# A fused long convolution and spectral mixing layer on one core: output tiles by threes ahead of two U tiles, and x's last piece in quarters

## The chip, the cores and the metric

The kernel runs on one core of one Trainium2 chip. The metric is the device time of one execution in microseconds (us). Three runs of the kernel before gave 373.09, 373.68 and 374.57 us, a median of 373.68. The execution that the profiler recorded took 373.66 us; its span, from the first to the last recorded work, is 371.9 us.

## The reference

Two layers follow one another. The first is a causal convolution of each channel of `x` (8 batches of 5696 positions and 128 channels) with a filter `h` as long as the sequence. The second is a Fourier mixing layer: the 64 lowest modes of the sequence are multiplied by complex 128 x 128 matrices and added back, and a gated linear map closes it.

```python
B, S, D = x.shape                      # 8, 5696, 128
L = 2 * S
Xf = np.fft.rfft(x, n=L, axis=1)
Hf = np.fft.rfft(h, n=L, axis=0)
x = np.fft.irfft(Xf * Hf[None], n=L, axis=1)[:, :S, :]       # the first layer

X = np.fft.rfft(x, axis=1)                                   # the second
Xr, Xi = np.real(X[:, :64]), np.imag(X[:, :64])
Yr = einsum('bmd,mde->bme', Xr, w_r) - einsum('bmd,mde->bme', Xi, w_i)
Yi = einsum('bmd,mde->bme', Xr, w_i) + einsum('bmd,mde->bme', Xi, w_r)
y = np.fft.irfft(Y, n=S, axis=1)       # Y holds Yr + i Yi in its first 64 modes
u = x + y
out = u + np.maximum(u @ w_ch, 0.0)
```

The result is 8 x 5696 x 128 in float32. All matmuls of the kernel take float16.

## The kernel before, in words

The sequence is cut as 5696 = 89 x 64, so that the long Fourier transform becomes two short ones, all done as matmuls with constant matrices. The eight batches are worked in four pairs, g = 0 to 3.

A recorder writes the program down first. Every operation is given an engine, the tokens that it reads and the tokens that it writes, and each engine runs its list strictly in the order of the recording; an operation waits on semaphores for the writers of what it reads and the readers of what it overwrites. There is no scheduler: the order of the recording calls is the order of the work on every engine. DMAs are recorded on the lists of SyncE or GpSimd and are issued when their turn comes. Most instructions carry the line of a helper in the profile: L330 is every matmul, L318 and L320 evictions on ScalarE, L322 and L324 evictions on VectorE, L327 every DMA.

The stages, in order:

- Start. The filter `h` and the first pair of `x` are loaded; `x` comes in eight pieces into the raw tiles `Xr`, each piece by two DMAs (L363). VectorE places each piece into `Xin` (function `x_place`, L370), where the 128 channels stand as four groups of 32 columns. Meanwhile TensorE transforms the filter (`a_tile`'s sister loop and `filter_couple`), and where it has nothing to do it runs matmuls on a constant whose result nobody reads (`idle`, L425). The eight `x_place` calls stand at L703, an `idle(18, 6)` at L707. Then 32 column tiles of `x` are transformed (`a_tile`, L466); tile j takes columns 4j to 4j + 3, all from the column group j // 8, but waits for all eight placed pieces as a whole (`XIN`).
- For each pair: the second short transform, the product with the filter's spectrum on VectorE, the third stage, which writes its results (`Zs`, `Zt`) to the scratch tensor `zscr` in HBM, and the 64 modes. Between two pairs the column tiles of the next one are worked.
- The modes are mixed with `W` and transposed into `C` (L820 to L847).
- The last stage, from 256 us of the span to its end, is where most of the change lies. A pair has 4 chunks of 16 rows for each of its 2 batches, and each chunk 2 halves: 16 U tiles per pair. A U tile (`u_tile`, L800) is 2 matmuls of 356 columns with `C` and 16 of 89 columns with the `zscr` data that was loaded back (tiles `ZT`, five chunk buffers), added up in two PSUM banks; one copy then moves it into `UT` on ScalarE or VectorE. When all 8 U tiles of a batch are there, the output tiles of that batch can be worked: 12 O tiles (`o_tile`, L857), 11 full ones with 512 positions and a short one with 64. A full O tile is 4 matmuls of 256 columns, whose right side `WI` is `w_ch` beside the identity; ScalarE takes the relu of one half into `R` (L886), VectorE adds the other half to it in float32 (L887), and SyncE stores it. Two O tiles side by side make one 512 KB store ("wide"); the eleventh full tile makes a store of 256 KB, the short one 32 KB.

U and O tiles share four PSUM slots of two banks each, taken in turn (`LSLOT = [0, 2, 4, 6]`). A tile can therefore start on TensorE only when the tile four before it has been read out: a U tile by its copy, an O tile by both the relu and the add.

The O tiles of one pair are worked between the U tiles of the next. Before, the loop at L903 put one O tile behind the first half of each chunk and two behind the second: U O U O O. For the last pair the batches come one after the other, with two O tiles behind each U tile and, for its second batch, two and three in turn; O tiles of the last pair's first batch join the list when its 8 U tiles are done. The last 12 O tiles follow the last U tile. Which engine copies a U tile out was counted off: five of eight on ScalarE, three on VectorE. When both batches of a chunk are done, its buffer is loaded again for the chunk five further on (`load_zt`, L913), after the O tiles of that chunk on SyncE's list.

Of the kernel before, what the change touches and what calls it, by code (L numbers as in the profile page):

```python
# [123 lines left out]
def bass_long_conv_fft__then__afno_spectral_mix_kernel(nc, x, h, moe_w_r, moe_w_i, moe_w_ch, out):  # L124
    B, S, D = x.shape
# [3 lines left out]
    NQ = S // J  # L129
# [12 lines left out]
    f1 = np.zeros((P, 2 * NK))  # L142
# [65 lines left out]
    def at(name, cols, dt, off):  # L208
        return nc.alloc_sbuf_tensor_at(name, [P, cols], dt, offset=off)
# [11 lines left out]
    XD = D // 4  # L221
    XE = XD + 2
    XQ = 2 * J * XE
    XW = 4 * XQ
    a_x = take(XW * 2)
    x_sb = at("Xin", XW, F16, a_x)
# [16 lines left out]
    XC = 4  # L243
    XN = J // XC
    XB = XN * D
    x_raw = [at(f"Xr{i}", XB, F16, a_as + 2 * HPW + 2 * XB * i if i < 7 else a_st + 2 * J * D) for i in range(2 * XC)]
# [15 lines left out]
    NC = 5  # L262
# [29 lines left out]
    def ap(t, row, p0, n, off, dims):  # L292
        return bass.AP(t, p0 * row + off, [[row, n]] + [list(d) for d in dims])
# [5 lines left out]
    def pv(bank, off, dims, p0=0, n=P):  # L299
        return bass.AP(ps, p0 * 4096 + bank * 512 + off, [[4096, n]] + [list(d) for d in dims])  # L300

    R = Recorder(nc)
# [3 lines left out]
    def bank(i):  # L306
        return ("bank", i)
# [21 lines left out]
    def mm(o, l, r, st, sp, reads, writes):  # L329
        R.add("tensor", lambda h_: h_.matmul(o, l, r, start=st, stop=sp), reads, writes)  # L330
# [3 lines left out]
    def once(key, toks):  # L334
        if key in first:
            return []
        first[key] = 1
        return list(toks)
# [3 lines left out]
    def turns(name, items):  # L342
        i = ring2.get(name, 0)
        ring2[name] = i + 1
        return items[i % len(items)]
# [24 lines left out]
    def x_place(i, src, toks):  # L370
        R.add("vector", lambda e: e.tensor_copy(bass.AP(x_sb, i * XN * XE, [[XW, NQ], [XE, XN], [XQ, 4], [1, XD]]),
                                                bass.AP(src, 0, [[XB, NQ], [D, XN], [XD, 4], [1, XD]])),
              list(toks) + XZ, [("xin", i)])

    def w_pieces():
        out_ = []
# [27 lines left out]
        return ((k // KP) ^ c) * MC + k % KP * 3 * J + (J if r == 0 else 0)  # L404

    XZ = [("xz", 0), ("xz", 1)]
    XIN = [("xin", i) for i in range(2 * XC)]
    XR = [[("xr", i, p_) for p_ in range(2)] for i in range(2 * XC)]
    GP = 2 * KT
    NS = NK // 2 + 1  # L410
# [14 lines left out]
    def idle(n, b0, w=512):  # L425
        for i in range(n):
            mm(pv(b0 + i % 2, 0, [[1, w]]), f1_sb[:, 0:P], ap(f1_sb, 2 * NK, 0, P, 0, [[0, w // P], [1, P]]),
               True, True, [("f1",)], [bank(b0 + i % 2)])
# [12 lines left out]
    for c_ in (0, 2, 1, 3):  # L441
        dst = bass.AP(hp_sb, c_ // 2 * J * HS + c_ % 2 * DC, [[HPW, NQ], [HS, J], [1, DC]])
        src = bass.AP(h_in, c_ * DC, [[J * D, NQ], [D, J], [1, DC]])
# [8 lines left out]
    for j in range(16):  # L452
        t = turns("h", [0, 2, 4, 6])
        for i in range(4):
            d = 4 * j + i
# [10 lines left out]
    def a_tile(j, slots, eng=None):  # L466
        t = turns("s", slots) if len(slots) > 1 else slots[0]
        for i in range(4):
            d = 4 * j + i
            mm(pv(t + i // 2, (i % 2) * 2 * NK, [[1, 2 * NK]]),  # L470
               ap(x_sb, XW, 0, P, d // XD * XQ + d % XD, [[XE, 2 * J]]), f1_sb[:, :], True, True,
               XIN + XZ + [("f1",), ("xc", d // XD)], [bank(t + i // 2)])
        if eng == "both":
            for i, e in enumerate(("vector", "scalar")):
                evac(bass.AP(a_sb, 4 * j + 2 * i, [[AW, P], [D, 2 * NK], [1, 2]]), pv(t + i, 0, [[1, 2 * NK], [2 * NK, 2]]),
                     [bank(t + i)], [("as", j + i)], 1.0 / 64, eng=e, after=once(("hp", j), HP))
            return
        evac(bass.AP(a_sb, 4 * j, [[AW, P], [D, 2 * NK], [2, 2], [1, 2]]),
             pv(t, 0, [[1, 2 * NK], [512, 2], [2 * NK, 2]]),
             [bank(t), bank(t + 1)], [("as", j)], 1.0 / 64, eng=eng, after=once(("hp", j), HP))  # L480
# [78 lines left out]
    V, A = "vector", "scalar"  # L559
# [140 lines left out]
    for c_ in range(NE):  # L700
        filter_couple(c_, turns("f", SLOTS[0:3]), "vector" if c_ == 1 else "scalar")
        idle(1, 6)
    for i in range(2 * XC):  # L703
        x_place(i, x_raw[i], XR[i])
    for i in (4, 5):
        m_cross(i, "gpsimd")
    idle(18, 6)  # L707
    load.update(scalar=0.0, vector=0.0)
    for j in range(32):
        a_tile(j, [turns("s", SLOTS)], "both" if j == 31 else share(720))  # L710
        if j >= 10 and j % 5 == 0:
            c_ = NE + (j - 10) // 5
# [8 lines left out]
    for g_ in range(NP):  # L721
# [27 lines left out]
        if g_ + 1 < NP:  # L749
            for j in range(4, 32):  # L750
# [3 lines left out]
                if wp and j > 4 and j % 2 == 1:  # L754
                    dst, src_, ring, tok = wp.pop(0)
# [11 lines left out]

    LSLOT = [0, 2, 4, 6]
    NCH = J // ZB
    n_ev = [0]  # L770
    ahead = {}

    def u_z(i, b, half, alone=False, parts=(0, 1)):
# [23 lines left out]
           ib_sb[:, (c_ * ZB + pl0) * NQ:(c_ * ZB + pl0 + 4) * NQ], first_, not first_,  # L797
           [("c", g_ // 2), ("ib", 0)] + ([("ib", 1)] if c_ >= NCH // 2 else []), [bank(t + hb)])

    def u_tile(i, b, half):  # L800
        g_, c_ = divmod(i, NCH)
        t = ahead.get((i, b, half))
        if t is None:
            t = u_z(i, b, half)
        else:
            for hb in range(2):
                u_c(i, b, half, t, hb, False)
        ub = (g_ % 2) * 2 + b
        old = {0: WT, 1: WT, 2: U_ALL, 3: U_ALL}[ub]
        n_ev[0] += 1  # L810
        e = "scalar" if n_ev[0] % 8 in (0, 2, 3, 5, 7) else "vector"
        src = pv(t, 0, [[1, NQ], [512, 2], [NQ, 4]])
        evac(bass.AP(u_sb[ub], c_ * ZB + half * 8, [[S, P], [J, NQ], [4, 2], [1, 4]]),
             src, [bank(t), bank(t + 1)], [("u_", ub, 2 * c_ + half)], eng=e, after=once(("u", ub), old))
# [39 lines left out]
    NW = S // P  # L854
    TAIL = S - NW * P

    def o_tile(g_, b, r4):  # L857
        ub = (g_ % 2) * 2 + b
        bb = 2 * g_ + b
        t = turns("l", LSLOT)  # L860
        i = n_o[0]
        n_o[0] += 1
        full = r4 < NW // 4
        last_ = (g_, b) == (NP - 1, 1)
        wide = r4 < (8 if last_ else NW // 4 // 2 * 2)
        big = wide or (last_ and full)
        h_ = r4 % 2 if wide else 0
        if big:
            if not h_:
                o_cur[0] = turns("o8", list(range(NO8)))  # L870
            ob, key, old = o8_sb[o_cur[0]], ("o8", o_cur[0]), o8_old[o_cur[0]]
        else:
            k_ = turns("os", list(range(NO)))
            ob, key, old = o_sb[k_], ("os", k_), o_old[k_]
        OW = 1024 if big else 512
        n, rows = (4, P) if full else (1, TAIL)
        rd = [("u_", ub, c_) for c_ in range(2 * NCH)] + [("wch",), ("i16",)]
        for j in range(n):
            lh = bass.AP(u_sb[ub], 4 * r4 + j, [[S, P], [NW, P]]) if full else u_sb[ub][:, NW * P:S]
            mm(pv(t + j // 2, (j % 2) * 256, [[1, 256]], 0, rows), lh, WI, True, True, rd, [bank(t + j // 2)])  # L880
        bk = [bank(t), bank(t + 1)] if full else [bank(t)]
        rs = r_sb[i % NR]
        rv = bass.AP(rs, 0, [[512, rows], [P, n], [1, P]])
        ov = bass.AP(ob, h_ * 512, [[OW, rows], [P, n], [1, P]])
        src_r, src_u = pv(t, 0, [[256, n], [1, P]], 0, rows), pv(t, P, [[256, n], [1, P]], 0, rows)
        R.add("scalar", lambda e: e.activation(rv, src_r, RELU), bk, [("r", i % NR)], after=once(("r", i % NR), G_ALL + XTT + [("y", q) for q in range(4)] + [("id",)]))  # L886
        R.add("vector", lambda e: e.tensor_tensor(ov, src_u, rv, ADD), bk + [("r", i % NR)],  # L887
              [key + (h_,)], after=once(key, old))
        if wide and not h_:
            return  # L890
        w_ = (2 if wide else 1) * 4 * D
        if full:
            dst = bass.AP(out.tensor, out.offset + bb * S * D + (4 * r4 - 4 * h_) * D, [[NW * D, P], [1, w_]])
            src = ob[:, 0:w_]
        else:
            dst = bass.AP(out.tensor, out.offset + bb * S * D + NW * P * D, [[D, TAIL], [1, D]])
            src = ob[0:TAIL, 0:P]
        dma("sync", dst, src, "o", [key + (v_,) for v_ in range(h_ + 1)])

    todo = []  # L900
    NB = NCH * NP
    NW4 = NW // 4 + 1
    for g_ in range(NP):  # L903
        last = g_ == NP - 1
        order = [(c_, b) for b in range(2) for c_ in range(NCH)] if last else [(c_, b) for c_ in range(NCH) for b in range(2)]
        for n, (c_, b) in enumerate(order):
            i = NCH * g_ + c_
            for half in range(2):
                u_tile(i, b, half)
                for _ in range((2, 2 + half)[n >= NCH] if last else 1 + half):  # L910
                    if todo:
                        o_tile(*todo.pop(0))
            if b == 1 and i + NC < NB:  # L913
                load_zt(i + NC)
            if last and n == NCH - 1:
                todo += [(g_, 0, r4) for r4 in range(NW4)]
        todo += [(g_, b, r4) for b in range(1 if last else 0, 2) for r4 in range(NW4)]
    while todo:
        o_tile(*todo.pop(0))
    R.add("sync", lambda e: e.nop(), [], [("o8", i, v_) for i in range(NO8) for v_ in range(2)] + [("os", i, 0) for i in range(NO)])  # L920
# [31 lines left out]
```

## Time and profile before

| what | before |
|---|---|
| median of three runs | 373.68 us |
| the profiled execution, its time | 373.66 us |
| its span | 371.9 us |
| TensorE busy, matmuls | 353.4 us, 95% |
| ScalarE busy | 312.5 us, 84% |
| VectorE busy | 300.6 us, 81% |
| GpSimd busy | 97.2 us, 26% |
| HBM read and written | 68.4 and 51.1 MB |

The busy shares are means over stages with different limits. Matmuls are pipelined, so the duration of one is longer than the distance to the next; where a rate matters, the distance between starts is read. PEld is the weight load that goes with each matmul, and runs ahead of it. In the rows of the timeline the first number is the start and the second the length in us; what stands in brackets is how long the engine was idle before it, and what released it.

### The profile page before, as it was taken

To read this page: it belongs to the slowest core of one execution; us is meant where nothing else is said; L and a number is where in the kernel's file an instruction comes from. 1 tells how busy PE (TensorE), PEld (TensorE's weight loads), DVE (VectorE), ACT (ScalarE), POOL (GpSimd) and SP (SyncE) were. 2 spreads that over 40 slices of the span, in tenths; PEclk is the share of its full clock that TensorE was granted. 3 is DMA by queue.
4 is the path that set the end of the run, shared out by engine and by line. 5 is a ranking of instruction groups with operands and counts; after the bars stand their busy time and mean duration, and the time that the engine had idled before them with its cause. 6 is when DMAs were issued, how large, how long until landed. Compare 5 with 4: busy or idle time off the path is not lost.

```text
span 371.9 us, 12188 instructions
## 1 busy us (share of the span) xinstructions
PE 353.4 (95%) x5222; PEld 268.0 (72%) x5222; DVE 300.6 (81%) x333; ACT 312.5 (84%) x492; POOL 97.2 (26%) x140
## 2 busy tenths in 40 slices
PE   7989989999999999899999899999999999999992
PEld 3756866667856668766668666668898898888872
DVE  7786988999889999889999987873356776778784
ACT  8875989999999999899999899994477767677783
POOL 8865013211922313723305204336000000000000
PEclk9999999999999999999999999999999999999998
DMA  7998579998999997999998989999999999998677
GB/s 141 285 221 219 117 163 254 279 254 235 144 142 239 249 256 159 151 164 236 250 267 131 360 236 341 349 314 367 401 399 374 403 420 406 405 403 357 275 276 297
DMA packets 84129, 101.71 MB, mean 273 GB/s; under 512 B 22078, under 2 KB 68926, under 8 KB 81106
## 3 DMA queue, kind: packets, MB, share of 16 engines
q1 hardware_dynamic: 59643, 67.73, 53.3%
q0 software_dynamic: 24432, 33.20, 43.4%
q8 instruction: 41, 0.67, 0.7%
q14 instruction: 13, 0.11, 0.1%
HBM read 68.38 MB, written 51.12 MB: 321 GB/s over the span
## 4 chain that ended last, share of the span: by engine, by line
PE 79%; ACT 13%; DMA 3%; DVE 2%; issue 1%; DVEq 0%; POOL 0%; POOLq 0%
PE ps L330 79%; ACT As L320 9%; DMA Hin<-in_h_dram 3%; DVE U L623 1%; ACT R L886 1%; ACT UT L318 1%; ACT Hp L445 1%; DVE Ah L324 0%; DVE UT L322 0%; ACT Ah L320 0%; ACT Hs L318 0%; DVE O L887 0%; DVEq L105 0%; POOL Hin L327 0%; ACT C L320 0%
## 5 line engine op out<-in xcount | busy, mean ns | idle before, releaser
L330 PE MATMUL ps<-U,Wc 128*128 128x512 f16 (+1 forms) x368 | 94.6, 376 | 0.0
L631 DVE TENSOR_TENSOR U<-Xs,Hs 128x2048 f16<-128x2048 f16 (+1 forms) x68 | 80.5, 1188 | 10.9 <-ACT Xs L318 8.8
L318 ACT CAST Xs<-ps 128x1024 f16<-128x1024 f32 (+1 forms) x72 | 69.5, 971 | 6.9 <-PE ps L330 4.7
L887 DVE TENSOR_TENSOR O<-ps,R 128x512 f32<-128x512 f32 x81 | 52.5, 686 | 20.4 <-ACT R L886 11.2
L318 ACT CAST Zs<-ps 128x512 f16<-128x512 f32 (+1 forms) x120 | 62.9, 600 | 0.4
L886 ACT ACTIVATE R<-ps 128x512 f32<-128x512 f32 x96 | 50.9, 573 | 14.4 <-PE ps L330 14.0
L324 DVE TENSOR_SCALAR As<-ps 128x720 f16<-128x720 f32 (+1 forms) x65 | 53.8, 881 | 4.6 <-PE ps L330 3.4
L330 PE MATMUL ps<-As,M 64*128 64x128 f16 x1440 | 48.7, 217 | 4.8 <-DVE U L623 3.5
L330 PE MATMUL ps<-WI,UT 128*128 128x256 f16 x360 | 51.7, 278 | 0.5 <-DVE O L887 0.4
L330 PE MATMUL ps<-F,Xin 128*128 128x180 f16 x512 | 51.3, 248 | 0.5 <-ACT As L320 0.2
L320 ACT ACTIVATE As<-ps 128x720 f16<-128x720 f32 (+1 forms) x67 | 46.3, 763 | 4.3 <-PE ps L330 4.0
L330 PEld LDWEIGHTS ps<-F,Xin 128*128 128x128 f16 x512 | 43.6, 142 | 8.4 <-ACT As L320 1.5
L330 PEld LDWEIGHTS ps<-U,Wc 128*128 128x128 f16 x368 | 28.4, 97 | 27.6 <-ACT Zs L318 4.8
L330 PEld LDWEIGHTS ps<-As,M 64*128 64x128 f16 x1440 | 40.3, 94 | 10.6 <-DVE U L623 4.2
L631 DVE TENSOR_TENSOR U<-ps,Hs 128x2048 f16<-128x2048 f32 x20 | 45.7, 2284 | 0.0
L318 ACT CAST UT<-ps 128x712 f16<-128x712 f32 x40 | 30.0, 752 | 17.4 <-PE ps L330 16.4
L327 POOL DMA_DIRECT2D Xt<-in_x_dram x48 | 24.7, 518 | 75.6 <-PE ps L330 74.9
L330 PEld LDWEIGHTS ps<-WI,UT 128*128 128x128 f16 x360 | 39.2, 152 | 4.1 <-issue 1.9
L330 PE MATMUL ps<-IBs,C 128*128 128x356 f16 x128 | 39.2, 314 | 0.8
L330 PEld LDWEIGHTS ps<-G,Zs 128*128 128x128 f16 x468 | 25.4, 96 | 12.0
L318 ACT CAST Zt<-ps 128x512 f16<-128x512 f32 (+1 forms) x64 | 33.8, 606 | 0.1
L322 DVE CAST UT<-ps 128x712 f16<-128x712 f32 x24 | 21.4, 891 | 9.5 <-PE ps L330 9.5
(90 smaller groups left out, 506.8 us busy)
## 6 DMA issues: line engine op xcount, KB each, us to landing
out_dram<-O SPq DMA_DIRECT2D x39, 512.0 KB, 7.4
zscr<-Zs SPq DMA_DIRECT2D x57, 256.0 KB, 6.0
zscr<-Zt SPq DMA_DIRECT2D x31, 256.0 KB, 7.3
Xt<-in_x_dram POOLq DMA_DIRECT2D x24, 320.0 KB, 6.5
W<-wscr POOLq DMA_DIRECT2D x8, 512.0 KB, 8.7
ZT0a<-zscr SPq DMA_DIRECT2D x3, 1024.0 KB, 9.8
Xr<-in_x_dram POOLq DMA_DIRECT2D x8, 320.0 KB, 15.9
M<-cM POOLq DMA_DIRECT2D x3, 720.0 KB, 12.8
```

What stands on the lines that cost most here:

```text
L318: R.add(e, lambda h_: h_.copy(dst, src), reads, writes, after=after)
L320: R.add(e, lambda h_: h_.activation(dst, src, COPY, scale=scale), reads, writes, after=after)
L322: R.add(e, lambda h_: h_.tensor_copy(dst, src), reads, writes, after=after)
L324: R.add(e, lambda h_: h_.tensor_scalar_mul(dst, src, scale), reads, writes, after=after)
L327: R.add(eng, lambda h_: h_.dma_start(dst, src), reads, writes, ring=ring, after=after)
L330: R.add("tensor", lambda h_: h_.matmul(o, l, r, start=st, stop=sp), reads, writes)
L445: R.add("scalar", lambda e, dst=dst, src=src: e.copy(dst, src), HT, [("hp", c_)])
L623: R.add("vector", lambda e, b=b, s_=s_: e.tensor_tensor(bass.AP(u_s[i], b * 512, [[2048, P], [1024, 2], [1, n * D]]), s_, hv, MULT), [tok, ...
L631: R.add("vector", lambda e: e.tensor_tensor(uv, src, hv, MULT), bk + [("h", t, 0), ("h", t, 1, 0), ("h", t, 1, J)], [("u", i)])
L886: R.add("scalar", lambda e: e.activation(rv, src_r, RELU), bk, [("r", i % NR)], after=once(("r", i % NR), G_ALL + XTT + [("y", q) for q in ...
L887: R.add("vector", lambda e: e.tensor_tensor(ov, src_u, rv, ADD), bk + [("r", i % NR)], [key + (h_,)], after=once(key, old))
```

## The change

Four things are changed, and one follows.

1. The last stage's order is written out. For pairs 1 to 3 as far as they work output tiles: three O tiles, then two U tiles (`PLAN`, with "A" a U tile copied by ScalarE and "V" one copied by VectorE). In pair 0 there are no O tiles yet, so its U tiles follow each other and alternate between the two engines. For the last pair the order is `LAST_PLAN`, with 12 groups of 2, 3 or 4 O tiles and one or two U tiles; 11 of its 16 U tiles are copied by ScalarE.
2. The reload of a chunk buffer is recorded directly behind the chunk's last U tile.
3. In the very last batch the ninth and tenth O tiles are stored as one wide pair like the others, and the short tile comes ahead of the eleventh.
4. The last of the eight pieces of the first `x` is placed in four quarters, one for each column group, by VectorE, ScalarE, VectorE and VectorE. A column tile waits only for the quarters of its own column group. The 18 `idle` matmuls ahead of the column tiles become 14.

```diff
     def x_place(i, src, toks):
...
-              list(toks) + XZ, [("xin", i)])
+              list(toks) + XZ, [("xin", i, q) for q in range(4)])
+
+    def x_quarter(i, q, eng, src, toks):
+        dst, s_ = bass.AP(x_sb, i * XN * XE + q * XQ, [[XW, NQ], [XE, XN], [1, XD]]), bass.AP(src, q * XD, [[XB, NQ], [D, XN], [1, XD]])
+        R.add(eng, (lambda e: e.copy(dst, s_)) if eng == "scalar" else (lambda e: e.tensor_copy(dst, s_)), list(toks) + XZ, [("xin", i, q)])
...
-    XIN = [("xin", i) for i in range(2 * XC)]
+    XIN = [[("xin", i, q) for i in range(2 * XC)] for q in range(4)]
...
-               XIN + XZ + [("f1",), ("xc", d // XD)], [bank(t + i // 2)])
+               XIN[d // XD] + XZ + [("f1",), ("xc", d // XD)], [bank(t + i // 2)])
...
-    for i in range(2 * XC):
+    for i in range(2 * XC - 1):
         x_place(i, x_raw[i], XR[i])
+    for q, e_ in enumerate(("vector", "scalar", "vector", "vector")):
+        x_quarter(2 * XC - 1, q, e_, x_raw[-1], XR[-1])
...
-    idle(18, 6)
+    idle(14, 6)
...
-    def u_tile(i, b, half):
+    def u_tile(i, b, half, e):
...
-        n_ev[0] += 1
-        e = "scalar" if n_ev[0] % 8 in (0, 2, 3, 5, 7) else "vector"
...
-        wide = r4 < (8 if last_ else NW // 4 // 2 * 2)
+        wide = r4 < NW // 4 // 2 * 2
...
+    PLAN = "OOOAV" * 8
+    LAST_PLAN = "OOOA" + "OOOAV" + "OOA" + "OOOAV" + "OOOOA" + "OOOAV" + "OOA" + "OOOAV" + "OOOOA" + "OOOAV" + "OOOA" + "OOO"
...
-        for n, (c_, b) in enumerate(order):
-            i = NCH * g_ + c_
-            for half in range(2):
-                u_tile(i, b, half)
-                for _ in range((2, 2 + half)[n >= NCH] if last else 1 + half):
-                    if todo:
-                        o_tile(*todo.pop(0))
-            if b == 1 and i + NC < NB:
+        us = [(NCH * g_ + c_, b, half) for c_, b in order for half in range(2)]
+        for step in (LAST_PLAN if last else PLAN):
+            if step == "O":
+                if todo:
+                    o_tile(*todo.pop(0))
+                continue
+            i, b, half = us.pop(0)
+            u_tile(i, b, half, "scalar" if step == "A" else "vector")
+            if b == 1 and half == 1 and i + NC < NB:
                 load_zt(i + NC)
-            if last and n == NCH - 1:
+            if last and len(us) == 2 * NCH:
                 todo += [(g_, 0, r4) for r4 in range(NW4)]
-        todo += [(g_, b, r4) for b in range(1 if last else 0, 2) for r4 in range(NW4)]
+        todo += [(g_, b, r4) for b in range(1 if last else 0, 2) for r4 in (list(range(NW4 - 2)) + [NW4 - 1, NW4 - 2] if last else range(NW4))]
```

More of the change, by code (lines that the diff above doesn't have):

```diff
@@ L769, in bass_long_conv_fft__then__afno_spectral_mix_kernel @@
     NCH = J // ZB
-    n_ev = [0]
     ahead = {}
```

## The prediction

> **What bounds the kernel now.** I read the two strips over the span first, then the chain of work that ended last, then windows by stage, then the engines' instructions in order of time at the three places that the edit touches.
>
> From the page: the strips of TensorE and of the DMA engines, and the chain's shares by engine.
> ```profile
> PE   7989989999999999899999899999999999999992
> ...
> DMA  7998579998999997999998989999999999998677
> ...
> PE 79%; ACT 13%; DMA 3%; DVE 2%; issue 1%; DVEq 0%; POOL 0%; POOLq 0%
> ```
> TensorE is full nearly throughout and carries 79% of the chain. A change must take time out of TensorE's stream.
>
> Windows: start and end, length, then busy us (and count) of PE, PEld, DVE, ACT, POOL, then granted clock, DMA share, GB/s. The first two are one half each of the pairs g = 1 and 2, the third is g = 3, the fourth the end.
> ```profile
> 284.00:297.40 13.40, 13.30 (x193) 11.85 (x190) 9.75 (x15) 9.64 (x18) 0.00 (x0) 1.00 1.01 387
> 297.40:310.80 13.40, 13.30 (x193) 11.87 (x191) 9.75 (x15) 9.64 (x19) 0.00 (x0) 1.00 1.02 411
> ...
> 324.00:359.00 35.00, 33.81 (x427) 28.91 (x425) 26.24 (x42) 25.54 (x48) 0.00 (x0) 1.00 0.83 332
> 359.00:372.00 13.00, 5.99 (x41) 4.47 (x41) 7.85 (x15) 6.52 (x12) 0.00 (x0) 0.90 0.78 299
> ```
> VectorE and ScalarE are 73% busy, TensorE 99%; the DMA engines are as full as TensorE, which becomes a rival below.
>
> One U tile and its output tiles on TensorE, ScalarE and VectorE, and the short output tile (64 rows) at the end of a half:
> ```profile
> 284.47 0.62 PE L330 MATMUL ps<-WI,UT 128*128 128x256 f16 x4
> 284.94 0.31 PE L330 MATMUL ps<-IBs,C 128*128 128x356 f16 x1
> 285.13 0.60 ACT L886 ACTIVATE R<-ps 128x512 f32<-128x512 f32 x1 [0.99 <-PE ps L330]
> 285.83 0.69 DVE L887 TENSOR_TENSOR O<-ps,R 128x512 f32<-128x512 f32 x1
> 285.91 1.06 PE L330 MATMUL ps<-WI,UT 128*128 128x256 f16 x8
> 286.81 0.31 PE L330 MATMUL ps<-IBs,C 128*128 128x356 f16 x1
> ...
> 283.10 0.11 PEld L330 LDWEIGHTS ps<-WI,UT 128*64 128x64 f16 x1 [0.16 <-issue]
> 283.46 0.10 PEld L330 LDWEIGHTS ps<-IBs,C 128*128 128x128 f16 x1 [0.26 <-issue]
> 327.37 0.10 PEld L330 LDWEIGHTS ps<-S4a,ZT2a 128*128 128x128 f16 x1 [0.78 <-issue]
> ```
> From one O tile's start to the U tile behind it is 0.47 us, from two 0.90. So an O tile costs 0.427 (4 matmuls 0.107 apart) and each turn from O to U another 0.045, however many O tiles stood before it. A U tile costs 0.983 (consecutive U tiles without O, 261.42 to 262.40 by their copies). The short tile costs 0.16 + 0.107 + 0.26 = 0.53. At 327.37 the stream paused 0.78 us with nothing shown that it waited for.
>
> The start (x's last piece and the dummy matmuls) and the end (the last store issues):
> ```profile
> 28.67 2.76 PE L330 MATMUL ps<-F 128*128 128x512 f16 x12 [0.44 <-issue]
> 30.24 0.69 DVE L371 COPY Xin<-Xr 89x2048 f16<-89x2048 f16 x1 [1.22 <-DMA Xr<-in_x_dram]
> 31.27 2.89 PE L330 MATMUL ps<-F,Xin 128*128 128x180 f16 x29
> ...
> 366.62 0.27 DVE L887 TENSOR_TENSOR Os<-ps,R 64x128 f32<-64x128 f32 x1
> 367.33 0.84 SPq L327 DMA_DIRECT2D out_dram<-O  x1
> 368.22 0.64 SPq L327 DMA_DIRECT2D out_dram<-Os  x1
> ```
> x's last piece lands at 30.24, is placed by 30.93, and the dummies run until 31.23: they end last, so today they hold the first matmul on x, at 31.27.
>
> **The change part by part.** The sum is made against the profiled execution, 373.66 us (span 371.9 and 1.8 around it); the median of the runs is 373.68, the same.
>
> *Start: quarters and four dummies less.* Four dummies at 2.76/12 = 0.21 each (by their spacing) would end at 30.38 instead of 31.23, before x is placed. What then ends last is the first quarter: landing 30.24, plus a copy of 512 elements per partition. No row shows it; below is a quarter of 0.69 = 0.17, above the 0.41 of the VectorE copy of 256 elements from PSUM. I take 0.24, near the lower end because source and target are the same as in the whole piece. Then 0.13 to the weight load (30.93 to 31.06 before) and 0.10 to the matmul: 30.71, against 31.27: **-0.55** (bounds -0.35 and -0.65). The ScalarE quarter is first needed by the ninth column tile, some 4 us later, and ScalarE is idle from 27.8 to 31.8, so it costs nothing; without that cover it would be one copy, under 0.6. VectorE does all three of its quarters by 31.0, before the first eviction that would fall to it (31.5). What could absorb the gain is the filter matmul at 35.50, which needs GpSimd's copy of M that ends at 34.5: 1.0 us of cover, so it stays. From there the chain is TensorE's.
>
> *Pairs 1 and 2: OOOUU instead of UOUOO.* The same tiles; per five-tile group one turn instead of two. A group becomes 3 x 0.427 + 0.05 + 2 x 0.983 = 3.30; a group with the short tile 2 x 0.427 + 0.53 + 1.97 = 3.35. A half of a pair: 3 x 3.30 + 3.35 = 13.25, against 13.42 now (283.46, 296.89, 310.31 mark the halves). That is -0.17, four times: **-0.7**. It needs that no tile waits for its PSUM slot. There are four slots in turn, so a tile needs the fourth one before it read out. With the group's first O tile at 0, the second U tile (from 2.31) needs that very O tile: its relu starts at 0.66 (284.47 to 285.13), ends 1.26, the VectorE add runs 1.36 to 2.05, and TensorE follows a release by 0.05 to 0.15: 2.20. Margin 0.1. The first U tile (from 1.33) needs the previous group's second U tile: ready 1.19 after its start at -0.99, copied by VectorE 0.89, to 1.09, free at 1.24. Margin 0.1. VectorE per group: three adds 0.605 apart and one U copy 0.80 = 2.6 of 3.3; ScalarE three at 0.49 and one at 0.65 = 2.1. Six to eight U copies per pair go to VectorE (0.89 each against 0.75 on ScalarE); both engines' idle time hides that, and what it costs without that cover is the margin above. Nothing below zero is excluded: if the margins are gone by 0.1, 20 such groups cost 2.
>
> *Queue order.* The load of the next z chunk is queued on SyncE right behind its last U tile, not behind two more O tiles. It waits for TensorE there, and the stores behind it belong to later O tiles, so they aren't held. The tightest chunk is the last: issued 319.30, landed 12.8 us later at 332.1, first used at 336.3: 4.2 us of cover, so zero; gone, it would be one wait of as much as the load is late.
>
> *Pair 3.* From the first U tile (323.77) to the half's short tile (357.94) is 34.17 us. The work in it: 16 x 0.983 + 33 x 0.427 + 2 x 0.53 + 0.16 and 16 turns = 31.75, so 2.4 us are waits: the pause of 0.78 and about 1.6 of slot waits of 0.15 to 0.3. With the written-out order there are 12 turns (-0.2). Its waits, by the same reckoning: where a group has one U tile only, the second and third O tiles of the next group stand four behind the second and third O tiles of the last one and wait 0.06 and 0.18, about four times, 1.0 in all. The groups of four O tiles each hold a short one (the 12th and 24th), so they add no more. 1.6 becomes 1.0: **-0.8** together. The pause I leave as it is.
>
> *The end.* The last twelve O tiles are held by the adds, 0.605 apart, as before. The short tile now stands ahead of the last full one, whose relu comes later because of it: the last add ends 0.2 later, measured from the previous short tile. Against that SyncE issues three stores instead of four behind 365.54, each 0.33 to 1.15 long in this stretch. Before, the last issue started 1.3 behind the last add and landed 3.2 later; now the 256 KB store starts some 0.5 behind it and lands 4.0 later (the row of such stores there). The DMA engines are over 0.97 busy from 366 to 370 either way. Together **-0.1** (bounds -0.6 and +0.5).
>
> Sum: -0.55 - 0.7 - 0.8 - 0.1 = -2.15: 373.66 - 2.15 = **371.5 us**.
>
> **The rivals.** A measurement of this kernel can't tell less than about 0.5% (1.9 us) from no change.
>
> *The DMA engines set the pace (no change).* A pair moves 4 chunks of 1440 KB in and 2 x 2848 KB out, 11.73 MB in 26.85 us, 437 GB/s wanted, against 387 to 411 moved at a share of 1.01. Store landings grow from 7.1 us (at 272) to 12.5 (at 320): the backlog is real. Against it: seven pair buffers come round after at least 15 O tiles, 5 groups, 16.5 us, and landings would grow by under 1 to 13.4. If the backlog did bind, pairs 1 and 2 gain nothing and pair 3 starts with the wait: -2.15 + 0.7 + 0.5 gives 372.7. [...]
>
> *The pause.* It is 0.78 once, and 0.44 at 28.2. If it falls away, 370.7; a second one, 372.3. The cause isn't in the trace, so either can be.
>
> *The margins of 0.1 don't hold (slower).* One mechanism: in OOOUU the second U tile waits for the first O tile's add. For: three adds and a U copy stand in VectorE's queue where three adds and 0.75 copies stood. Against: add and relu durations vary by under 0.02 (680 to 694 ns). If the add ends 0.35 later than reckoned, 0.24 of it counts in each of 20 groups: +4.8 - 2.15 gives 376.3. It decides from 0.21 later on.
>
> *The start is held by something else.* If x lands later or the placed quarter isn't what ends last, -0.55 goes: 372.1.
>
> **How the numbers follow.** Forecast (371.5, own range 370.8 to 372.2): 0.50. Pause gone: 0.15. DMA pace: 0.12. Start held: 0.10. Second pause: 0.03. Margins gone: 0.10. The bound of -0.5% is 371.8. Of the forecast's own spread about 0.45 in 0.50 lie below it, as do all of "pause gone"; the rest, but the slow case, lie within 0.5%: faster 0.60, same 0.30, slower 0.10. The range leaves out the slow case and the far end of the pause: 370.2 to 373.0.
>
> **What would show it.** First matmul on x at 30.7 (was 31.27), with no dummy up to it. Halves of pairs 1 and 2 13.25 apart, TensorE idle only around the short tile. Pair 3 33.4 long or, without the pause, 32.6. One pair store, the short one, one of 256 KB at the end. It's wrong if weight loads of U tiles show regular waits on VectorE, if adds wait for stores, or if the halves stay 13.4 apart at a DMA share of 1.0.

## The result, and the profile after

Four runs of the changed kernel gave 368.99 to 371.52 us, a median of 369.6; four of the kernel before beside them gave 373.09 to 374.57, a median of 373.61. The ratio is 0.9898, with a 95% interval of 0.9878 to 0.9918: faster by 1.0%, some 4.0 us. A second series gave 370.15 against 374.22, 0.9884 (0.9859 to 0.9910). The forecast was 371.5: the sign was right, the gain nearly twice what was forecast, and the time lies 0.6 us below the range. The profiled execution of the changed kernel took 369.91 us, with a span of 368.1 (before 371.9).

From the page of the changed kernel, the strips of TensorE and of the DMA engines, and the chain's shares by engine:
```profile
PE   7988989999999999899999899999999999999993
...
DMA  8997669998999996999997989999999999999877
...
PE 83%; ACT 12%; DVE 2%; issue 1%; DMA 0%; DVEq 0%
```
The picture is as before: TensorE's stream sets the time, and carries 83% of the chain instead of 79.

Windows of the changed kernel, with the columns of the first windows above: two halves, each from one short output tile to the next, then the last pair from its first O tile to the short tile of its first batch, then the end.
```profile
281.00:294.10 13.10, 13.10 (x191) 11.91 (x191) 10.73 (x16) 8.97 (x18) 0.00 (x0) 1.00 1.02 411
294.10:307.20 13.10, 13.10 (x191) 11.91 (x190) 10.73 (x16) 8.96 (x18) 0.00 (x0) 1.00 1.02 411
322.30:354.40 32.10, 32.10 (x427) 28.93 (x423) 25.32 (x39) 24.88 (x45) 0.00 (x0) 1.00 0.88 355
355.00:368.00 13.00, 6.25 (x43) 4.48 (x41) 8.35 (x15) 6.88 (x14) 0.00 (x0) 0.93 0.81 312
```
A half takes 13.10 us instead of 13.42, the last pair 32.0 instead of 34.2; VectorE is busy for 10.7 of the 13.1 us, where it was 9.75 of 13.4.

In the last pair, two of the long waits of TensorE's weight loads before, then one of the longest of the changed kernel:
```profile
346.82 0.10 PEld L330 LDWEIGHTS ps<-IBs,C 128*128 128x128 f16 x1 [0.31 <-ACT UT L318]
349.30 0.10 PEld L330 LDWEIGHTS ps<-IBs,C 128*128 128x128 f16 x1 [0.30 <-DVE UT L322]
```
```profile
325.63 0.44 PEld L330 LDWEIGHTS ps<-WI,UT 128*128 128x128 f16 x4 [0.16 <-ACT UT L318]
```
A third one of before stands at 353.98 (0.31). In the changed kernel's last pair four waits of 0.16 are all that brackets show.

The short tile in the order of time: weight loads of two short tiles (128x64) and, between them, of the U tile behind the first; then TensorE's matmuls behind the first short tile.
```profile
280.75 0.11 PEld L330 LDWEIGHTS ps<-WI,UT 128*64 128x64 f16 x1 [0.16 <-issue]
280.98 0.10 PEld L330 LDWEIGHTS ps<-IBs,C 128*128 128x128 f16 x1
293.85 0.11 PEld L330 LDWEIGHTS ps<-WI,UT 128*64 128x64 f16 x1 [0.16 <-issue]
```
```profile
280.98 0.32 PE L330 MATMUL ps<-IBs,C 128*128 128x356 f16 x1
281.97 0.31 PE L330 MATMUL ps<-IBs,C 128*128 128x356 f16 x1
282.95 1.50 PE L330 MATMUL ps<-WI,UT 128*128 128x256 f16 x12
```
The short tiles stand 13.10 apart. The 0.16 ahead of the tile is still there. Of the 0.26 behind it about half is gone: the U tile's weight load starts 0.23 behind the short tile's, where it was 0.36 (283.10 to 283.46). Some 0.12 of idle time stay, too short to be put in brackets. The two U tiles take 0.99 and 0.98.

The start, TensorE's matmuls and the copies of x's last piece:
```profile
29.48 1.90 PE L330 MATMUL ps<-F 128*128 128x512 f16 x8 [1.07 <-issue]
31.22 2.97 PE L330 MATMUL ps<-F,Xin 128*128 128x180 f16 x30
30.39 0.69 DVE L377 COPY Xin<-Xr 89x512 f16<-89x512 f16 x3 [1.15 <-DMA Xr<-in_x_dram]
```
The first quarter was in place by about 30.6, but the dummies still ended last: the pause among them took 1.07 us instead of 0.44. The first matmul on x came at 31.22, not at 30.7.

The end, SyncE's issues and VectorE's adds from 356 us on:
```profile
357.77 5.12 SPq L327 DMA_DIRECT2D out_dram<-O  x5
362.93 0.59 SPq L327 DMA_DIRECT2D out_dram<-Os  x1
363.58 1.19 SPq L327 DMA_DIRECT2D out_dram<-O  x1
362.44 0.27 DVE L890 TENSOR_TENSOR Os<-ps,R 64x128 f32<-64x128 f32 x1
362.83 0.69 DVE L890 TENSOR_TENSOR O<-ps,R 128x512 f32<-128x512 f32 x1
```
The short tile's store is now ahead of the 256 KB one, which goes out 0.06 us behind the last add.

Between the two profiled executions the span lost 3.8 us: 0.2 up to the copy of `C` (ScalarE's starts at 255.52 instead of 255.72), 1.3 in the four halves of pairs 1 and 2 (4 x 0.32), 2.15 in the last pair (34.17 to 32.0, of which 0.78 is the pause of before), 0.15 behind its short tile (13.93 to 13.78).

### The profile page after: what moved, and what is told of

It reads as the page before. It is cut to its first block, busy times and chain, and to the rows that moved or that the text cites. A ratio compares the mean times of both kernels' runs of the same rounds, so it can differ in the third digit from the quotient of the medians.

```text
span 368.1 us, 12186 instructions
## 1 busy us (share of the span) xinstructions
PE 350.7 (95%) x5218; PEld 268.2 (73%) x5218; DVE 306.1 (83%) x340; ACT 309.5 (84%) x488; POOL 96.8 (26%) x140
## 4 chain that ended last, share of the span: by engine, by line
PE 83%; ACT 12%; DVE 2%; issue 1%; DMA 0%; DVEq 0%
PE ps L330 83%; ACT As L320 10%; DVE U L627 1%; ACT R L889 1%; DMA F<-cF 0%; DVE O L890 0%; DVE Ah L324 0%; ACT Ah L320 0%; ACT Hs L318 0%; ACT UT L318 0%; ACT C L320 0%; PE ps L844 0%; DVEq L115 0%
## 5 line engine op out<-in xcount | busy, mean ns | idle before, releaser
L635 DVE TENSOR_TENSOR U<-Xs,Hs 128x2048 f16<-128x2048 f16 (+1 forms) x68 | 80.5, 1188 | 10.7 <-ACT Xs L318 9.6
L889 ACT ACTIVATE R<-ps 128x512 f32<-128x512 f32 (+1 forms) x96 | 48.6, 573 | 16.4 <-PE ps L330 16.0
L890 DVE TENSOR_TENSOR O<-ps,R 128x512 f32<-128x512 f32 x81 | 51.3, 685 | 10.4 <-ACT R L889 6.7
L330 PE MATMUL ps<-WI,UT 128*128 128x256 f16 x360 | 48.0, 277 | 0.9 <-DVE O L890 0.8
L318 ACT CAST UT<-ps 128x712 f16<-128x712 f32 x35 | 26.2, 752 | 16.1 <-PE ps L330 15.8
L322 DVE CAST UT<-ps 128x712 f16<-128x712 f32 x29 | 26.1, 899 | 13.9 <-PE ps L330 13.6
```

The costliest lines, as they stand in the source:

```text
L318: R.add(e, lambda h_: h_.copy(dst, src), reads, writes, after=after)
L322: R.add(e, lambda h_: h_.tensor_copy(dst, src), reads, writes, after=after)
L635: R.add("vector", lambda e: e.tensor_tensor(uv, src, hv, MULT), bk + [("h", t, 0), ("h", t, 1, 0), ("h", t, 1, J)], [("u", i)])
```

## The experiments

Theory A, the one on record: the gain is the sum of fewer turns between O and U tiles, of some slot waits of the last pair, and of x's start. Theory B, formed after the result: the 0.26 us behind the short tile is no cost of that tile but a wait of the U tile behind it for its PSUM slot, and the new order takes it away. Theory C: the even split of the U copies between the engines, not the order, makes the gain. A fourth question is what the pauses are, at the start and in the last pair. All ratios stand against the kernel before in the same series.

### The parts one at a time

The kernel before with the written-out order, its engine letters and the earlier reload alone:

```diff
+    PLAN = "OOOAV" * 8
+    LAST_PLAN = "OOOA" + "OOOAV" + ...
...
-        e = "scalar" if n_ev[0] % 8 in (0, 2, 3, 5, 7) else "vector"
...
+            u_tile(i, b, half, "scalar" if step == "A" else "vector")
```

> The kernel before with the written-out order alone (threes ahead of two U tiles, the last pair's list, the earlier reload); x's last piece whole, 18 dummies, the end's stores as before. If the order of the tiles is where the time went: 3.2 to 3.7 us faster than before (370.0 or so), halves of pairs 1 and 2 13.10 apart, almost all of the changed kernel's gain. If the start gives 0.55 as forecast and the order the rest: 2.9 us faster at the least, with about 0.6 missing against the changed kernel.

Measured: 370.34 us, 0.9906 (0.9893 to 0.9920). Of the 1.0 to 1.2% that the whole change brings, the order alone makes 0.9. Weight loads ahead of the first short tiles:
```profile
281.52 0.11 PEld L330 LDWEIGHTS ps<-WI,UT 128*64 128x64 f16 x1 [0.16 <-issue]
294.62 0.11 PEld L330 LDWEIGHTS ps<-WI,UT 128*64 128x64 f16 x1 [0.16 <-issue]
```
The halves are 13.10 apart here too, and 34.27 us lie between the short tiles of pair 2's end and of the last pair's first batch (320.82 and 355.09; 34.25 in the changed kernel).

The kernel before with the quarters and the 14 dummies alone:

```diff
-    idle(18, 6)
+    for q, e_ in enumerate(("vector", "scalar", "vector", "vector")):
+        x_quarter(2 * XC - 1, q, e_, x_raw[-1], XR[-1])
...
+    idle(14, 6)
```

> The kernel before with x's last piece in quarters and 14 dummies, nothing else. If the pause in the run of dummies and the dummies themselves hold the first matmul on x (as the changed kernel's trace shows, 31.22 against 31.27): 0.0 to 0.3 us faster, first matmul on x between 30.6 and 31.3 depending on the pause. If the changed kernel's trace caught an unusually long pause: 0.55 us faster as forecast, first matmul at 30.7.

Measured: 372.91 us, 0.9974 (0.9960 to 0.9987): a gain of 0.5 to 1.5 us, which holds the forecast of 0.55 at its edge. In the profiled execution x's last piece was late, and TensorE waited 1.16 us for the first quarter, until 31.96; from this trace the gain can't be read.

The kernel before with the last batch's stores and tile order alone:

```diff
-        wide = r4 < (8 if last_ else NW // 4 // 2 * 2)
+        wide = r4 < NW // 4 // 2 * 2
...
+        todo += [... (list(range(NW4 - 2)) + [NW4 - 1, NW4 - 2] if last else range(NW4))]
```

> The kernel before with the last wide store pair and the short tile ahead of the last full tile, nothing else. Forecast: 0.1 us faster (between 0.6 faster and 0.5 slower). If fewer store issues shorten the end, the last SyncE issue ends over 0.5 us sooner after the last add than before (1.97) and the time falls by 0.5.

Measured: 373.71 us, 0.9994 (0.9977 to 1.0011): no change that can be told, as forecast (-0.1). Its trace shows the last pair of the old order without a pause: 33.4 us (324.00 to 357.37).

The three parts add up to 1.0 + 3.6 + 0.2 = 4.8 us by their medians, against 4.0 and 4.1 for the whole; the intervals of the parts (about half a us each way) leave room for both.

### Slot wait or shape

Theory B says that the U tile behind the short one waits for the add of the O tile four before it. In the trace of before that add ran from 282.65 to 283.34, and the U tile's weight load began at 283.46, 0.12 later:
```profile
282.65 0.69 DVE L887 TENSOR_TENSOR O<-ps,R 128x512 f32<-128x512 f32 x1 [0.68 <-ACT R L886]
```
If the short tile stands one place earlier, the same U tile should still wait, behind a full tile; if the 0.26 comes from the tile's shape, it should move along with the tile.

```diff
-        todo += [(g_, b, r4) for b in range(1 if last else 0, 2) for r4 in range(NW4)]
+        todo += [(g_, b, r4) for b in range(1 if last else 0, 2) for r4 in (range(NW4) if last else list(range(NW4 - 2)) + [NW4 - 1, NW4 - 2])]
```

> The kernel before, with the short O tile ahead of the last full one in every half but the very last, so that the U tile follows a full O tile. If the 0.26 ahead of the weight load behind the short tile is the U tile's wait for its PSUM slot (the O tile four before it): a wait of 0.2 to 0.3 stays ahead of the U tile's first weight load, none stands directly behind the short tile's, and the halves stay at 13.4. If it is the cost of the short tile's shape: a wait of 0.26 stands directly behind the short tile, ahead of the last full O tile's weight load, and none ahead of the U tile.

Measured: one run at 373.66 us, the kernel before at 374.08. Weight loads of the short tile (with those of the full O tile behind it, in one row) and of the U tile that follows, twice; then the add of the O tile four before the first of these U tiles:
```profile
296.95 0.67 PEld L330 LDWEIGHTS ps<-WI,UT 128*64 128x64 f16 x5
297.78 0.10 PEld L330 LDWEIGHTS ps<-IBs,C 128*128 128x128 f16 x1 [0.17 <-issue]
310.38 0.66 PEld L330 LDWEIGHTS ps<-WI,UT 128*64 128x64 f16 x5
311.21 0.10 PEld L330 LDWEIGHTS ps<-IBs,C 128*128 128x128 f16 x1 [0.17 <-issue]
```
```profile
296.97 0.69 DVE L887 TENSOR_TENSOR O<-ps,R 128x512 f32<-128x512 f32 x1 [0.68 <-ACT R L886]
```
The result lies between the two expectations. The row of five weight loads takes 0.67 us, where a short tile's one (0.11) and a full tile's four (0.44) make 0.55: some 0.12 of idle time went along with the short tile. The rest stays with the U tile, which now follows a full tile, at 0.17; its weight load begins at 297.78, again 0.12 behind the end of the add (297.66). The halves are 13.43. So the 0.26 was two things: about 0.12 that goes with the short tile, with a U tile or a full O tile behind it, and about 0.14 that was the U tile's wait for its slot. "issue" in brackets does not exclude a slot: the trace names no releaser here, and the add fits by its time in both programs. The swap is one run, and the reading rests on its trace, not on its time.

### Order or engines

The order of before with the U copies alternating between the engines:

```diff
-        e = "scalar" if n_ev[0] % 8 in (0, 2, 3, 5, 7) else "vector"
+        e = "scalar" if n_ev[0] % 2 else "vector"
```

> The kernel before with its own order, only the U copies alternate between ScalarE and VectorE instead of five to three. If the order is the cause: within 0.6 us of before, halves of pairs 1 and 2 at 13.3 to 13.5 us. If the even split of the copies is the cause: 2 us faster or more, halves near 13.1.

Measured: 375.0 us, 1.0023 (1.0004 to 1.0043): slower if anything. The halves are 13.47, 0.04 longer. The even split has no worth of its own in the old order. The trace has a pause of 1.6 us in the last pair, on TensorE's unchanged program:
```profile
330.62 0.10 PEld L330 LDWEIGHTS ps<-S4a,ZT2a 128*128 128x128 f16 x1 [1.61 <-issue]
```

The changed kernel with the U copies counted off five to three as before, in the new order:

```diff
+    n_ev = 0
...
-            u_tile(i, b, half, "scalar" if step == "A" else "vector")
+            n_ev += 1
+            u_tile(i, b, half, "scalar" if n_ev % 8 in (0, 2, 3, 5, 7) else "vector")
```

> The changed kernel with its U copies counted off five to three as before, its order kept. If the order alone is the cause: within 0.5 us of the changed kernel (1.0% faster than before). If one U copy on each engine is needed: in groups with both copies on ScalarE or with the first one on VectorE relu or add come late for a slot, 0.1 to 0.3 us in about half of the 20 groups, 1 to 3 us slower than the changed kernel (0.2 to 0.7% faster than before).

Measured: 370.75 us, 0.9895 (0.9851 to 0.9938), not to be told from the changed kernel by its time. By its trace the halves are 13.26 apart, and the last pair has waits that the changed kernel lacks, as ahead of this U tile:
```profile
326.93 0.10 PEld L330 LDWEIGHTS ps<-IBs,C 128*128 128x128 f16 x1 [0.30 <-DVE UT L322]
```
In the changed kernel's trace a VectorE copy of a U tile takes 899 ns against 752 on ScalarE, and the wait above names one. Theory C falls: the order makes the gain. In this one trace the changed kernel's own letters are worth 0.15 us a half and 1.0 in the last pair (35.3 against 34.25 between short tiles), and the timings can't tell that.

The changed kernel with the last pair's order and letters as before:

```diff
-        for step in (LAST_PLAN if last else PLAN):
+        for step in ("VOOAOOAOOVOOAOOVOOAOOAOOVOOAOOOAOOVOOOAOOVOOOAOOAOOO" if last else PLAN):
```

> The changed kernel with the last pair's order and engines as before, pairs 1 and 2 by threes. By the changed kernel's trace pairs 1 and 2 give 1.3 us, the start 0.2 to 0.6, the last pair 1.4 and a pause of 0.8 that need not come: so 1.5 to 2.0 us faster than before (0.40 to 0.55%), the last pair 33.4 us long from its first U tile to its short tile. If pairs 1 and 2 gave only the forecast 0.7: 0.9 to 1.3 us.

Measured: 371.92 us, 0.9939 (0.9918 to 0.9960), against 0.9884 and 0.9898 for the changed kernel: the last pair's list is worth 1.5 to 2 us by the medians. The gain left over is 2.2 us, a little above the 1.5 to 2.0 expected. Between the short tiles (319.75 and 355.52) lie 35.8 us instead of 34.25. Two waits of its last pair:
```profile
328.03 0.10 PEld L330 LDWEIGHTS ps<-IBs,C 128*128 128x128 f16 x1 [0.42 <-ACT UT L318]
333.86 0.10 PEld L330 LDWEIGHTS ps<-IBs,C 128*128 128x128 f16 x1 [0.40 <-issue]
```
No pause stands in this trace, so these 1.5 us are slot waits and turns, without the pause.

### The start: dummies and the pause

The changed kernel again, and with 8 and with 4 dummies in place of 14:

```diff
-    idle(14, 6)
+    idle(8, 6)
```
```diff
-    idle(14, 6)
+    idle(4, 6)
```

> The changed kernel with 8 dummies ahead of the column tiles instead of 14. If pause and dummies hold the first matmul on x: it starts 0.3 to 0.35 behind the landing of x's last piece, at 30.7 to 30.8 when that lands at 30.4, and the time falls by 0.2 to 0.5 us against the changed kernel (about 1.1% faster than before). If the landing of x already sets the start in most executions: no change against the changed kernel.

> The changed kernel itself once more, beside the two variants of its dummies: 0.9 to 1.2% faster than before. Its trace shows whether the pause among the dummies at 28.4 us and the landing of x's last piece (30.2 to 31.7 in the traces so far) change from execution to execution: the first matmul on x at the later of the dummies' end and 0.35 behind the landing.

> The changed kernel with 4 dummies ahead of the column tiles instead of 14. If the dummies matter only as cover: first matmul on x 0.35 behind the landing of x's last piece, time as with 8 dummies (0 to 0.5 us faster than the changed kernel). If a longer idle stretch of TensorE lowers its granted clock: the windows behind 30 us show a clock under 1.00 and the column tiles run slower, 1 us or more lost.

Measured: 8 dummies 369.27 us, 0.9864 (0.9825 to 0.9903); 14 again 370.15, 0.9884 (0.9859 to 0.9910); 4 dummies 370.87, 0.9914 (0.9883 to 0.9945). The three can't be told apart. TensorE's matmuls and the first copy with 8 dummies:
```profile
29.75 0.60 PE L330 MATMUL ps<-F 128*128 128x512 f16 x2 [0.84 <-issue]
32.03 1.15 PE L330 MATMUL ps<-F,Xin 128*128 128x180 f16 x12 [1.67 <-DVE Xin L377]
31.68 0.69 DVE L377 COPY Xin<-Xr 89x512 f16<-89x512 f16 x3 [1.20 <-DMA Xr<-in_x_dram]
```
And TensorE's with 4:
```profile
30.93 3.26 PE L330 MATMUL ps<-F,Xin 128*128 128x180 f16 x33 [2.67 <-DVE Xin L377]
```
With 8 dummies x landed at 31.68 and its first matmul followed 0.35 behind; with 4 it landed at 30.59 and the matmul followed 0.34 behind. So the step from landing through the quarter to the matmul costs 0.35, where the forecast had 0.47; but the landing itself moves between 30.2 and 31.7 from run to run, more than all the start could gain. With 4 dummies TensorE stood idle for 2.67 us, and the granted clock of that execution was 0.994, as in the profiled repeat of the changed kernel. That doesn't settle the second expectation: this execution was the fastest of the six, their granted clocks over the whole execution were 0.988 to 0.994 (0.994 to 0.997 with 14 dummies), and the slower ones had the lower clock.

In every trace with so many dummies the pause stood behind the 13th, counted from the first of the seven that stand between the filter matmuls (18 or 14 more follow); with 4 there are only 11, and none was seen. To see whether that is a matter of the dummies between the filter matmuls, they were moved to the end (the same number in all ahead of the pause):

```diff
     for c_ in range(NE):
         filter_couple(c_, ...)
-        idle(1, 6)
...
-    idle(14, 6)
+    idle(21, 6)
```

> The changed kernel with the 7 single dummies between the filter matmuls taken out and 21 instead of 14 ahead of the column tiles, so that the first matmul on x has the same number of TensorE instructions ahead of it. If the pause is tied to a place in TensorE's instruction stream: it comes behind the 14th dummy or so instead of the 7th, with the filter matmuls themselves running without it. If it is tied to a moment (the DMA traffic at 28 us): it comes at 28.2 to 28.6 again.

Measured: one run at 369.17 us. TensorE's matmuls:
```profile
25.56 2.98 PE L330 MATMUL ps<-F 128*128 128x512 f16 x13
29.46 1.90 PE L330 MATMUL ps<-F 128*128 128x512 f16 x8 [0.93 <-issue]
31.20 2.97 PE L330 MATMUL ps<-F,Xin 128*128 128x180 f16 x30
```
Again behind the 13th, but at the same time as before, 28.5, since the work ahead of it was the same. Place and time were parted by making the dummies narrower, so that the 13th comes earlier:

```diff
-    idle(21, 6)
+    idle(60, 6, P)
```

> The kernel after, with the seven single dummies between the filter matmuls removed as in the run just before and, in place of the 21 dummies of 512 columns, 60 of 128 columns, so that the 13th dummy is issued at about 26.3 us instead of 28.3. In every trace so far the pause stood behind the 13th dummy, which always came at about 28.3. If the place is given by the number of instructions issued alone: the pause begins at about 26.3, and it is about 1 us long if its length is its own, or it lasts to about 29.4 (3 us) if what TensorE waits for then is something that arrives at a set time. If it is given by the time alone: the dummies run on past the 13th and stop at about 28.4. In each case the first matmul on x stays at 30.7 to 31.3, held by x's placed quarter or by the dummies, since the pause and the dummies are over by then; if x lands late, by as much later. Time within 0.5% of the kernel after.

Measured: one run at 371.35 us, span 369.6. TensorE's matmuls:
```profile
25.42 0.90 PE L330 MATMUL ps<-F 128*128 128x128 f16 x13
29.21 4.42 PE L330 MATMUL ps<-F 128*128 128x128 f16 x47 [2.90 <-issue]
33.47 4.26 PE L330 MATMUL ps<-F,Xin 128*128 128x180 f16 x44
```
The pause begins at 26.3, still behind the 13th dummy, and lasts 2.9 us, until 29.21: in this run its place is given by the number of instructions, its end by something that arrives at a set time. The second part of the expectation missed: the 47 dummies left ran 0.09 apart, not 0.07, ended at 33.5 and held x's first matmul, 2.25 later than in the changed kernel. That miss was in the experiment's size, and its time says nothing of the change.

What arrives can be seen in the DMA queues. In the stretch from 26.7 to 26.8 of this run, the rows by queue (packets, MB, share of 16 engines):
```profile
q8 instruction: 1, 0.02, 60.9%
```
One packet of instructions; the 41 packets of this queue in the trace of before are 16 KB each (0.67 MB). Read in the same way, in stretches of 0.1 us, for other kernels of the series (the stretch with the packet, and the end of the pause):

| kernel | packet | TensorE goes on | behind it |
|---|---|---|---|
| before, start | 26.2 | 28.67 | 2.5 |
| order alone, start | 26.7 | 29.21 | 2.5 |
| old last pair, start | 26.8 | 29.22 | 2.4 |
| changed kernel, start | 27.2 | 29.48 | 2.3 |
| 8 dummies, start | 27.2 | 29.75 | 2.6 |
| dummies moved, start | 27.0 | 29.46 | 2.5 |
| narrow dummies, start | 26.7 | 29.21 | 2.5 |
| before, last pair | 324.9 | 327.37 | 2.5 |
| engines alone, last pair | 328.2 | 330.62 | 2.4 |

In all nine TensorE goes on 2.3 to 2.6 us behind a packet of instructions, and so it does at the start of the six other traces with that many dummies. In the narrow run the pause grew by as much as TensorE came earlier. That it waits there for its next instructions is the author's reading, which fits all of them. It was not shown: the row doesn't name the engine that the packet is for, and no run moved the packet itself. In the last pair of the old order the place of the pause lies near the end of the second U tile. TensorE comes to it 1.7 and 0.7 us behind the packet in the two traces that pause, and 2.5, 2.7, 2.7 and 5.7 behind it in the four that don't (the start's part alone, the end's part alone, the short tile moved, the old last pair in the changed kernel).

Pauses of this kind were seen at two places only. They took 0.44 to 1.07 us at the start (2.9 with the narrow dummies), and 0.78 and 1.6 in the last pair. Between the packet and TensorE's next matmul the DMA share was 1.03 (start) and 1.04 (last pair) in the trace of before, and 1.00 (start) in that of the changed kernel.

## Why the prediction was right and wrong

- **The sign and what bounds the kernel: right.** TensorE's stream set the time before and after, and the gain came out of it.
- **Pairs 1 and 2, -0.7: the mechanism was right, and one term of it was mis-sized.** This is the step that failed: "The short tile costs 0.16 + 0.107 + 0.26 = 0.53". Of the 0.26 only about 0.12 goes with the short tile; the other 0.14 was the wait of the U tile behind it for its PSUM slot, which the forecast carried along as fixed work and the new order takes away. The run with the short tile moved parts the two. With 0.39 for the short tile the working gives 8 x 0.983 + 11 x 0.427 + 0.39 + 3 x 0.045 = 13.09 for a half, against 13.10 measured and 13.25 forecast. Four times 0.32 was gained, not four times 0.17: 0.6 of the miss.
- **The last pair, -0.8: its slot waits were mis-sized, too.** Without the pause the gain was 1.4 (33.4 to 32.0). With 0.39 for each of its two short tiles the working gives 31.5 of work before and 31.3 after. So the waits were 1.9 and became 0.8: 1.1 less, where 0.6 less was forecast (1.6 to 1.0). Only one of the two short tiles had a U tile's long wait behind it (0.28, at 336.27); behind the other a full O tile followed, with some 0.12 of idle time before and after. The waits of 0.30 and 0.31 shown above went as well, and four of 0.16 stay. How they share the 1.1 is read from two traces; no run took them apart. The list has 11 turns from O to U tiles where the working had 12, which is 0.05.
- **The pause, left as it is: it went in the profiled execution.** That is 0.78 of the difference between the two spans. It comes and goes with TensorE's program unchanged, so it should not be credited to the change; the traces of the old last-pair order hold it in two of six (0.78 and 1.6), those of the new order in none. Whether the new order hinders it or these runs were lucky isn't settled.
- **The start, -0.55: not in the profiled execution, and not contradicted by the timings.** The trace shows -0.05 at x's first matmul, since the pause grew to 1.07 and the dummies ended last once more; the rival that the start is held by something else had the right mechanism for this one execution. Alone the part gained 0.5 to 1.5 us. In the five traces with the quarters and 14 dummies x's first matmul came at 30.93, 30.95, 31.20, 31.22 and 31.96; in the five with the whole piece and 18 dummies between 31.27 and 32.05, with a median of 31.55. That is some 0.35 by the medians.
- **The end, -0.1: not contradicted** (-0.15 in the trace, 0.9994 with 0.9977 to 1.0011 alone). Executions differ by more than this at the end.
- **Queue order, zero: right.** No load of a chunk was waited for.
- **Margins of 0.1 don't hold: fell.** They held: the view shows no wait on VectorE in the halves. They are thin, though: with the copies counted as before the halves are 13.26, and behind a short tile nothing is left of the margin, since the U tile at 280.98 starts 0.12 behind the end of VectorE's copy (280.86).
- **The DMA engines set the pace: fell.** From 300 to 330 us the wide stores landed 11.7 us behind their issue, 11.3 before, and the DMA engines moved 409 GB/s at a share of 1.02 (411 at 1.02 before). No add waited for a store: from 260 to 355 us the waits ahead of the adds into `O` ended with ScalarE (6.7 us) or TensorE (3.5). The halves shrank all the same.
- **The range.** It ended at 370.2 because the pause was priced alone (370.7), with the sum of the slot terms taken as known. The sum had no bounds of its own for the short tile: 0.14 at each of five places makes -0.7, by which the sum would have been 370.8, and 370.0 without the pause. The two were never laid together. That this comes close to the profiled 369.91 is in part luck, since the gain that the start lacked and the further slot waits of the last pair about cancel.

## What to carry to other kernels

A gap beside an odd-shaped tile isn't all a cost of its shape until the wait has been followed to its slot: count back as many tiles as there are buffers, and compare the end of that tile's read-out with the next start, also where the trace writes "issue". When an order of tiles is changed, list every wait of the old order and work out for each whether its slot partner moves; a wait carried along as fixed work hides the gain. A pause on a full engine with nothing to wait for can be looked up in the instruction queue's packets, and, if it ends the same time behind one in every trace (2.3 to 2.6 us here), it shouldn't be counted for or against a change.

## What was not expected of the hardware

- At the start TensorE stopped behind the same dummy in every kernel that had it ahead of x's first matmul, and went on 2.3 to 2.6 us behind a 16 KB packet of instructions; a stream that came to the place 2 us earlier only waited 2 us longer (2.9 instead of 0.9).
- x's last piece landed between 30.2 and 31.7 us with the same loads ahead of it.
- From the end of the last add to the end of the span it took 4.6 us in both executions of the changed kernel, and between 3.3 and 5.2 in the six variants of it with the same last stores: executions differ by some 2 us here as well, and a single trace decides nothing below that.
